# Attention and MLP on one core: the order of the first loads, with two w_out pieces and batch 1's first q and k between w_in's third and fourth piece

## The chip, the cores and the metric

The kernel runs on one core of a Trainium2 chip. A core has five engines with a queue of instructions each: TensorE (PE: matmuls, with PEld for its weight loads), VectorE (DVE), ScalarE (ACT), GpSimd (POOL) and SyncE (SP, which here issues nearly all DMAs). Each queue is worked off in order; semaphores make an instruction wait for another engine's or for a DMA. The metric is the device time of one execution in microseconds (us), less is better.

## The reference

Two layers in a row. The first is attention over 8 batches, 8 heads, 576 positions and 64 dimensions, with a window: heads 0 to 3 see the last 32 positions, heads 4 to 7 (dilated) every fourth of the last 128. The second takes the heads of a position as a row of 512 and applies two matrices with a leaky ReLU between them.

```
scores = where(mask[h], q @ k.T / 8, -1e9)        # rel = query - key
mask[h < 4]  = (0 <= rel < 32)
mask[h >= 4] = (0 <= rel < 128) & (rel % 4 == 0)
x   = softmax(scores) @ v                          # 8 x 8 x 576 x 64
x   = x.transpose(0, 2, 1, 3).reshape(4608, 512)
h   = x @ w_in                                     # 512 x 2048
out = maximum(0.01 * h, h) @ w_out                 # 2048 x 512
```

All inputs and the output are float32; the kernel computes in fp16 with float32 sums.

## The kernel before

The 4608 rows are worked in 12 chunks of 384 (three to a pair of batches). A chunk goes *up*: 16 blocks j of 128 hidden units, each four matmuls over the 512 inputs (`up`, L1112, matmuls at L1128), evicted by ACT with the leaky ReLU into `gt` (L1139). Then it goes *down*, 128 rows at a time. The first four row tiles are done plainly (`down`, L1288): four groups of four matmuls, 128x512 (L1299). All others go four tiles at a time in `group` (L1341), which computes a two by two block product with seven products for eight; its matmuls are L1390. The last four chunks do the same on the way up (`up_seven`, L1168, matmuls L1212). Both need sums and differences of weight quarters (`weight_sums`, L1325, with L1329 for w_out; `up_sums`, L1154, for w_in), 128x2048 each on DVE.

Batches 0 and 1 (`EARLY`) are done in a form of their own: q and k are loaded in rows, cast to fp16 (L345 on POOL and DVE, L343 on ACT), turned by PE (L783) and copied into `slots` (L698 on ACT, L700 on DVE). A `unit` (L896) then has scores (L924, L943, L927), an exponential on ACT (L949), for some a mask on DVE (L960), the product with the values (L984, L994, L1004, and L972 for the row sums), logarithm and exponential for the reciprocal (L1016, L1018) and the norm into `xt` (L1022). The first 512 positions of a batch are "part 0", the last 64 of each head the remainder ("part 1", loaded by `load_rest`, L544). Chunk 0 is batch 0's part 0, chunk 1 batch 1's, chunk 2 the two remainders. The other six batches (`late_unit`, L1031: scores L1065, mask L1081, sums and values L1071, norm L1100) are turned by DVE (L751, L771, L776) with copies on POOL (L739).

Weights come as float32 pieces of 512 KB (`load_w`, L611): w_in in eight, w_out in eight, each cast to fp16 by two or four casts. Pieces are staged in buffers that are used later for other things: w_in's first two in `gt[2]`, the third and fourth in `wst[0]`, then `gt[1]` and `xt[1]`; w_out's first in `xt[1]`, the second and third again in `wst[0]` (so they wait for the casts of w_in's third and fourth), the rest again in `gt[1]` and `xt[1]`. The first four pieces of w_in make the left half of the hidden units: pieces one and two the first two of the four input blocks, three and four the last two.

What sets the order is a planner that runs when the kernel is built. Every instruction is a task with a guessed duration for each engine that may take it (`add`, L84; loads with a guessed service time, `load`, L330). `_Plan.run` (L106) places tasks on engines by readiness and priority; `latest` (L169) goes backwards over the result and makes each task's due time its new priority, and the two are repeated once for each entry of `SEEDS`, an entry other than zero adding random shifts. The planned order is then fixed in every engine's queue. SP's loads keep a priority of their own: `FIRST` (L26) is a string that is read from left to right (L1518 to L1526): `b` and `c` are q and k of a group of four heads of batch 0 and 1, `v` and `y` their values, `i` a piece of w_in, `o` a piece of w_out, `0` and `1` the remainders. A load waits for what last used its buffer, and each of SP's DMAs also waits for the DMA eight places before it, for they share eight semaphores. Where the plan leaves PE idle before `WARM`, filler matmuls on zeros are put in (L1616; the first eight are at L1509).

These are the lines in which the list's costs of w_in's first pieces and of the remainder stand:

```
    def load(queue, dst, src, n, size, deps, prio, slow=1.0):
        ...
        return plan.dma(queue, 0.7 if n == 1152 else 0.62 if over == 64 else 0.45, took(n, size) * slow, deps,
...
        t = load("SP", st, dram(moe_w_in, n % 4 * 128 * DFF + x, [DFF, 128], [1, 1024]), 128, 4096, old, prio,
                 W_SLOW if n < 4 else 1.0)
```

`WHEN` and `RANKS` are first priorities of the batches' attention, `MOE` the pitch of the chunks' first priorities, `W_SUMS` and `SUMS` those of the weight sums.

Of the kernel before, what the change touches and what calls it, by code (L numbers as in the profile page):

```python
# [16 lines left out]
LATE = 7.0  # L17
HOLD = 5.0
W_ENG = ("POOL", "DVE", "ACT")
WHEN = (31.41, -0.6, 17.98, 85.1, 92.7, 99.49, 158.42, 166.15)  # L20
WARM = 62.0
W_SLOW = 1.5
SEEDS = (0, 0, 0, 0, 0, 0, 0, 0, 206472, 469597)
AFTER = -1495.0
NEAR = -1482.0
FIRST = "bvbviiii0iiiicoocoyoooooy1"  # L26
RANKS = ((24.53, -24.71), (34.17, 3.07), (0.12, 16.48), (29.7, 7.1))


def _constants():  # L30
# [47 lines left out]
class _Plan:  # L78
# [11 lines left out]
    def shared(self, *args):  # L90
        t = self.add(*args)
        t.port = True
        return t
# [117 lines left out]
def kernel(  # L211
# [43 lines left out]
    def at(tl, p0, p1, off, *dims):  # L255

        row = tl.ap[0][0]
        return bass.AP(tensor=tl.tensor, offset=tl.offset + p0 * row + off,
                       ap=[[row, p1 - p0]] + [list(d) for d in dims])

    def dram(t, off, *dims):
        return bass.AP(tensor=t.tensor, offset=t.offset + off, ap=[list(d) for d in dims])
# [67 lines left out]
    def load(queue, dst, src, n, size, deps, prio, slow=1.0):  # L330
        eng = ENG[queue]
        over = getattr(src if prio == -3000 else dst, "ap", [[0, 0]])[0][1]
        return plan.dma(queue, 0.7 if n == 1152 else 0.62 if over == 64 else 0.45, took(n, size) * slow, deps,
                        lambda e: eng.dma_start(dst, src), prio,
                        LATE if prio > -1500 + len(FIRST) else 0.8 if prio >= AFTER else 0.0)

    def cast(dst, src, n, deps, prio, engines=("POOL",)):
        cost = {"POOL": 0.05 + n * (0.00118 if n <= S else 0.00104), "DVE": 0.1 + n * 0.00053,
                "ACT": 0.06 + n * 0.00087}

        def fn(e):
            if e == "ACT":
                nc.scalar.copy(out=dst, in_=src)  # L343
            else:
                ENG[e].tensor_copy(out=dst, in_=src)  # L345
        return shared(tuple((e, cost[e]) for e in engines), None, 0.2, deps, fn, prio, 0.0, "cast")
# [6 lines left out]
    def ring(name, n, users):  # L353

        r = rings.setdefault(name, [])
        waits = r[-n] if len(r) >= n else []
        r.append(users)
        return (len(r) - 1) % n, waits
# [23 lines left out]
    def clear_slots(slots, prio, deps):  # L382
        for i in slots:
            t_zero[i] = ([clear("DVE", qbd[i][64:128, 0:S], 0.34, 0.0, prio, deps),
                          clear("DVE", qbd[i][0:64, S:2 * S], 0.34, 0.0, prio, deps)],
                         [clear("DVE", kt[i][:, 0:PAD], 0.1, 0.0, prio, deps)])
# [157 lines left out]
    def load_rest(b, prio):  # L544


        _, r_old = ring("REST", 1, r_users := [])
        sn, s_old = ring("STG", NST, s_users := [])
        st, lo = stg[sn], []
        for o, src in ((0, q), (1, k)):  # L550
            lo.append(load("SP", at(st, 0, 128, o * 256, [1, 256]),
                           dram(src, b * H * HS + 512 * D, [HS, 8], [4 * D, 16], [1, 256]),
                           128, 1024, s_old, prio, 1.8))
        c = cast(at(rest, 0, 128, 0, [128, 8], [D, 2], [1, D]),
                 at(st, 0, 128, 0, [D, 8], [0, 2], [1, D]), 1024, lo + r_old, prio, W_ENG)
        s_users.append(c)
        vs, v_old, v_users = v_late[b]
        spread = bass.AP(tensor=vs.tensor, offset=vs.offset + 1024,
                         ap=[[4 * vs.ap[0][0], 16], [256, 4], [1, 256]])
        lv = load("SP", spread,  # L560
                  dram(v, (b * H + 4) * HS + 512 * D, [4 * D, 16], [HS, 4], [1, 256]),
                  64, 1024, v_old + [t_vr], prio)
        if b in SEL:
            ps, p_old, p_users = v_late[b, "plain"]
            lp = [load("SP", at(ps, 0, 128, 1024 + 256 * i, [D, 4], [1, D]),
                       dram(v, b * H * HS + (352 + 96 * i) * D, [D, 128], [HS, 4], [1, D]), 512, 256, p_old, prio)
                  for i in range(2)]
            for j in range(2):
                vt, d_users = kept[b, j]
                c_p = cast(at(vt, 0, 128, 512, [768, 2], [128, 2], [1, D]),  # L570
                           at(ps, 0, 128, 1024 + D * j, [2 * D, 2], [256, 2], [1, D]), 256, lp + d_users, prio, W_ENG)
                p_users.append(c_p)
                picked[b, j, 2] = [c_p]
        for vi in (2, 3, 0, 1):
            vt, d_users = kept[b, vi]
            c_v = []
            if vi >= 2:
                c_v = [cast(at(vt, 0, 64, 0, [1024, 2], [128, 4], [1, D]),
                            at(vs, 0, 64, 1024 + (vi - 2) * 256, [512, 2], [D, 4], [1, D]), 512,
                            [lv] + d_users, prio + 30, W_ENG)]  # L580
                v_users += c_v
            visits[b, vi, 1] = rest, [c], r_users, vt, c_v + seen_ones[b, vi], d_users
# [28 lines left out]
    def load_w(n, prio):  # L611
# [6 lines left out]
        if n >= 8:  # L618
            x = 1024 * (n - 8)
            t = load("SP", st, dram(moe_w_out, 128 * x, [2 * DM, 128], [1, 1024]), 128, 4096, old, prio)  # L620
            for i in range(2):
# [6 lines left out]
        t = load("SP", st, dram(moe_w_in, n % 4 * 128 * DFF + x, [DFF, 128], [1, 1024]), 128, 4096, old, prio,  # L628
                 W_SLOW if n < 4 else 1.0)
        g, h = n % 4 // 2, n % 2  # L630
# [15 lines left out]

    segs = {b: [(0, 96, 384 * (b % 2)), (96, 48, 768 + 192 * (b % 2))] for b in range(EARLY)}
    chunks = [(m, 384 * i, 384) for m in range(B // 2) for i in (0, 1, 2)]
    MOE = 36.66
    PLAIN = 4  # L650
    tiles = [(c, tt) for c in range(len(chunks)) for tt in range(3)]
    groups = [tiles[i:i + 4] for i in range(PLAIN, len(tiles), 4)]
# [1 line left out]
    for m, x, n in chunks:  # L654
        begins.append(begins[-1] + MOE * n / 384)

# [488 lines left out]
        return t_p  # L1145

    SEVEN = (8, 9, 10, 11)
    W_SUMS = 539.34
    u_sums, u_last = {}, {}

    def w_quarter(k, f):
# [2 lines left out]
    def up_sums(old, raw):  # L1154
# [3 lines left out]
        def make(n, dst, x, y, op, deps):  # L1158
            u_sums[n] = shared("DVE", 1.16, 0.2, deps,
                            lambda e: ENG[e].tensor_tensor(out=dst, in0=x, in1=y, op=op),  # L1160
                            W_SUMS, 0.0, "T")
        w_all = [c for j in range(NJ) for b in w_in_t[j] for c in b]
# [154 lines left out]
    def w_block(k, n):  # L1317
        return at(w_out, 0, 128, k * HJ * DM + n * HN, [DM, HJ], [1, HN])

    def flat(tl):  # L1320
        return at(tl, 0, 128, 0, [HN, HJ], [1, HN])
# [3 lines left out]
    def weight_sums():  # L1325
        w_all = sum((w_out_t[j] for j in range(NJ)), [])

        def minus(n, dst, x, y, deps):
            t_sum[n] = shared("DVE", 1.16, 0.2, deps, lambda e: nc.vector.tensor_tensor(  # L1329
                out=dst, in0=x, in1=y, op=ALU.subtract), SUMS, 0.0, "T")  # L1330
        minus(1, flat(sums[1]), w_block(0, 1), w_block(0, 0), w_all + w_used[9] + w_used[10])
# [4 lines left out]

    roles = [0, 1]
    last_of = {}
    SUMS = -123.87

    def group(four, acts, at_time, split):  # L1341

# [175 lines left out]
    ranks = {}  # L1518
    for n, step in enumerate(FIRST):
        seen = FIRST[:n].count(step)  # L1520
        if step in "io":
# [14 lines left out]
    def attend(b, part, first, step):  # L1536
        units = {None: (0, 1), 0: (0, 1), 1: (2,)}[part]
        if part == 1:
            load_rest(b, ranks[b])
        for n, hp in enumerate((2, 3, 0, 1)):  # L1540
            if part != 1 and n % 2 == 0:
                load_group(b, hp // 2, *(ranks[b, hp // 2, i] if b < EARLY else tick()
                                         for i in (0, 1)))
            if part == 0 and b in SEL and hp == 0:
                for u in units:
                    pick_values(b, u, first + step * n)
            got = turn(b, hp, part or 0, first + step * n)
            for u in units:
                if part is None:
                    late_unit(b, hp, u, got, first + step * n)  # L1550
                else:
                    unit(b, hp, part, u, got, first + step * n)
# [3 lines left out]
    for m in range(B // 2):  # L1556
        for b in (2 * m, 2 * m + 1):
            if b < EARLY:
                attend(b, 0, *RANKS[2 * b])
                if b == 0:  # L1560
# [3 lines left out]
                    clear_slots(range(4, NT), -700, x_done[0, 0][-1:])  # L1564
                attend(b, 1, *RANKS[2 * b + 1])
            else:
                a, z = WHEN[b - 1], WHEN[b]
                attend(b, None, a, (z - a) / 4)
# [40 lines left out]
    order = plan.run()  # L1609
    for seed in SEEDS:  # L1610
        plan.latest(seed)
# [67 lines left out]
```

## Time and profile before

| | |
|---|---|
| median of 3 runs | 307.46 us (307.44 to 307.6) |
| the profiled execution | 307.5 us |
| its span, first to last instruction | 305.7 us |
| granted TensorE clock | 1.00 |
| PE busy | 293.6 us, 96% |
| DVE, ACT, POOL busy | 247.8, 223.9, 123.2 us |
| read from and written to HBM | 37.25 MB, 9.44 MB |

How to read it: a row of a timeline has the start in us, the time it took, engine, line, operation, tiles and shapes, how many instructions were merged, and in brackets the idle time before it and what ended it. Busy time of PE counts filler as well, and matmuls overlap in the pipeline: eight of 128x384 that stand in a row are busy for 1.46 us but take 1.30 us of the chain. The profile's order by time has the loads first (DMA at 277 to 405 GB/s up to 40 us), the two early batches and chunk 0 up to 60 us, and from 70 us on matmuls back to back.

### The profile page before, as it was taken

Reading aid. Unit: us, or ns where it says so; the run is one execution under the profiler, and the core shown is the slowest. Engines: PE = TensorE matmul, PEld = TensorE weight load, DVE = VectorE, ACT = ScalarE, POOL = GpSimd, SP = SyncE. Lnnn points to the kernel's source line nnn. Section 1 sums busy time; section 2 is a strip of 40 time slices with the busy share of each in tenths; the row PEclk is TensorE's granted clock in tenths of the full one; section 3 lists DMA queues with packets and bytes.
Section 4 is the critical chain, followed back from the end, with each engine's and each line's share of the span. In section 5 each row is a group of like instructions: output and inputs, shape, how many; then the busy total and the mean of one; then the engine's idle time right before and its main releaser. Section 6 shows DMA issues by size and latency. Waiting matters only on the chain.

```text
span 305.7 us, 8137 instructions
## 1 busy us (share of the span) xinstructions
PE 293.6 (96%) x3050; PEld 231.4 (76%) x3050; DVE 247.8 (81%) x480; ACT 223.9 (73%) x547; POOL 123.2 (40%) x170
## 2 busy tenths in 40 slices
PE   8788899899999999999999999999999999999994
PEld 4445564466989678778877778778999999999984
DVE  5777868656999987999997889999999568677842
ACT  5788995597897885876778688577878768767420
POOL 6355862139908908954944753781000000000000
PEclk9999999999999999999999999999999999999999
DMA  7999988799897897848794988791211310031034
GB/s 244 405 362 376 405 270 147 178 174 203 169 190 151 149 169 161 147 115 145 161 160 134 166 173 162 143 199 46 72 36 34 101 41 0 2 105 36 2 109 133
DMA packets 155671, 47.23 MB, mean 154 GB/s; under 512 B 135408, under 2 KB 153072, under 8 KB 155632
## 3 DMA queue, kind: packets, MB, share of 16 engines
q1 hardware_dynamic: 155056, 46.39, 63.4%
q8 instruction: 24, 0.39, 0.5%
q10 hardware_dynamic: 576, 0.32, 0.4%
q14 instruction: 15, 0.12, 0.1%
HBM read 37.25 MB, written 9.44 MB: 153 GB/s over the span
## 4 chain that ended last, share of the span: by engine, by line
PE 78%; ACT 10%; DVE 7%; DMA 2%; issue 2%; SPq 1%; ACTq 0%
PE hps L1128 22%; PE fps L1390 21%; PE tp L1390 8%; PE hps L1212 7%; PE ops L1071 4%; PE ops L1212 3%; PE fps L1299 3%; DMA stg<-in_q_dram 2%; ACT gt L1139 2%; PE sps L1212 2%; ACT slots L698 2%; ACT ee L949 2%; ACT rc L1016 1%; DVE ee L1081 1%; PE sps L1071 1%
## 5 line engine op out<-in xcount | busy, mean ns | idle before, releaser
L1128 PE MATMUL hps<-xt,w_in 128*128 128x384 f16 (+1 forms) x556 | 98.5, 307 | 0.8 <-ACT gt L1139 0.7
L1390 PEld LDWEIGHTS <-gt 128*128 128x128 f16 x768 | 72.6, 98 | 8.8 <-DVE gt L1376 0.2
L1139 ACT ACTIVATE gt<-hps 128x384 f16<-128x384 f32 (+1 forms) x139 | 62.9, 457 | 21.8 <-PE hps L1128 20.3
L1128 PEld LDWEIGHTS <-w_in 128*128 128x128 f16 x576 | 49.9, 98 | 22.3 <-issue 1.7
L1390 PE MATMUL fps<-w_out,gt 128*128 128x256 f16 x368 | 47.0, 272 | 0.0
L739 POOL COPY slots<-turned 64x512 f16<-64x512 f16 (+1 forms) x36 | 27.7, 769 | 42.8 <-DVE turned L751 30.3
L345 POOL CAST v_all<-vst 64x1152 f16<-64x1152 f32 (+4 forms) x30 | 35.2, 1175 | 8.8 <-DMA vst<-in_v_dram 8.4
L345 POOL CAST nat<-stg 128x576 f16<-128x576 f32 (+1 forms) x46 | 34.9, 783 | 6.9 <-DMA stg<-in_q_dram 3.3
L1100 DVE TENSOR_TENSOR xt<-ops,rc 128x288 f16<-128x288 f32 x48 | 26.7, 557 | 5.7 <-PE ops L1071 3.1
L1081 DVE TENSOR_TENSOR ee<-ee,late_m 128x384 f16<-128x384 f16 (+1 forms) x48 | 27.1, 575 | 3.8 <-ACT ee L1078 3.2
L1212 PEld LDWEIGHTS <-w_in 128*128 128x128 f16 x256 | 21.9, 98 | 0.4
L1092 ACT ACTIVATE rc<-rc 128x288 f32<-128x288 f32 x48 | 21.2, 449 | 0.5
L1419 ACT COPY stg<-fps 128x512 f32<-128x512 f32 (+1 forms) x25 | 13.4, 534 | 10.6 <-PE fps L1390 10.2
L771 DVE STREAM_TRANSPOSE slots<-nat 64x576 f16<-64x576 f16 x24 | 18.4, 768 | 0.4
L751 DVE STREAM_TRANSPOSE turned<-nat 128x576 f16<-128x576 f16 (+1 forms) x24 | 17.5, 734 | 0.7 <-POOL slots L739 0.5
L1071 PEld LDWEIGHTS <-v_all 128*128 128x128 f16 x240 | 14.4, 98 | 3.9 <-issue 0.9
L1071 PE MATMUL ops<-ee,v_all 128*128 128x96 f16 (+2 forms) x240 | 16.4, 199 | 0.6 <-DVE xt L1100 0.6
L1212 PEld LDWEIGHTS <-stg 128*128 128x128 f16 x192 | 16.5, 98 | 0.3
L1299 PE MATMUL fps<-w_out,gt 128*128 128x512 f16 x64 | 16.2, 379 | 0.6 <-DVE w_out L345 0.6
L1390 PE MATMUL fps<-wst,gt 128*128 128x256 f16 x128 | 16.4, 272 | 0.0
L1071 PEld LDWEIGHTS <-sides 128*128 128x128 f16 x240 | 13.8, 97 | 3.0 <-issue 0.3
L1390 PE MATMUL tp<-w_out,gt 128*128 128x256 f16 x120 | 15.6, 273 | 0.0
(159 smaller groups left out, 593.9 us busy)
## 6 DMA issues: line engine op xcount, KB each, us to landing
stg<-in_q_dram SPq DMA_DIRECT2D x48, 144.0 KB, 3.5
stg<-in_k_dram SPq DMA_DIRECT2D x48, 144.0 KB, 3.0
vst<-in_v_dram SPq DMA_DIRECT2D x12, 288.0 KB, 4.0
vst<-in_v_dram SPq DMA_DIRECT2D x26, 128.0 KB, 2.8
gt<-in_moe_w_in_dram SPq DMA_DIRECT2D x5, 512.0 KB, 6.7
xt<-in_moe_w_out_dram SPq DMA_DIRECT2D x3, 512.0 KB, 9.0
gt<-in_moe_w_out_dram SPq DMA_DIRECT2D x3, 512.0 KB, 9.0
out_dram<-osb SPq DMA_DIRECT2D x9, 128.0 KB, 2.1
```

What stands on the lines that cost most here:

```text
L345: ENG[e].tensor_copy(out=dst, in_=src)
L739: lambda e: (nc.scalar.copy if e == "ACT" else nc.gpsimd.tensor_copy)(out=at(to, p0, p1, p0 if to is qb else 0, *dims), in_=at(fr, p0, p1, ...
L771: lambda e, p0=64 * h: nc.vector.transpose(at(qb, p0, p0 + 64, p0, [128, 9], [1, 64]), na[p0:p0 + 64, S:2 * S]), prio))
L1071: nc.tensor.matmul(at(bk, 0, 128, o, *dims), stationary(s), et[:, c:c + n], start=i == 0, stop=i == len(parts) - 1, skip_group_check=True)
L1081: lambda e: nc.vector.tensor_tensor(out=et[:, 0:w], in0=et[:, 0:w], in1=mk, op=ALU.mult), prio + 0.1)
L1092: lambda e: nc.scalar.activation(out=rt[:, 0:NQ], in_=rt[:, 0:NQ], func=AF.Exp, scale=-1.0),
L1100: lambda e: nc.vector.tensor_tensor(out=dst, in0=at(ot, 0, 128, 0, *src), in1=at(rt, 0, 128, 0, *src), op=ALU.mult), prio + 0.2)
L1128: nc.tensor.matmul(ht[:, 0:n], at(w_in, 0, 128, i * DFF + j // 2 * 256 + j % 2, [2, 128]), at(xt[m % 2], 0, 128, i * 1152 + x0 + x, [1, n] ...
L1139: lambda e: nc.scalar.activation(out=gt[c % NG][:, j * n_c + x:j * n_c + x + n], in_=ht[:, 0:n], func=AF.Prelu, alpha=0.01),
L1212: nc.tensor.matmul(bk[:, 192 * jj:192 * jj + 192], w(i, 2 * jp + jj), x(i), start=first and jj == 0 and i == 0, stop=jj == 1 and i == 1, s ...
L1299: nc.tensor.matmul(ft, g[:, j * n_c + tt * 128:j * n_c + tt * 128 + 128], w_out[:, j * DM:j * DM + DM], start=(j == 0), stop=(j == NJ - 1))
L1390: nc.tensor.matmul(bk[:, x:x + HN], tl[:, off + j * step:off + j * step + 128], rhs(j), start=first and x == 0 and j == 0, stop=j == HJ - ...
```

## The change

Constants alone change. The string of loads is another one: after the third `i` come two `o`, one `c`, then the fourth `i` and the remainder of batch 0, and the rest of w_in and w_out alternate. On SP's queue as built, w_out's first piece and batch 1's q and k of the dilated heads stand ahead of w_in's fourth piece; w_out's second piece, which must wait for the casts of w_in's third, stands behind w_in's fifth. Batch 1's plain values stand ahead of w_out's last two pieces, no longer behind them. The list's cost of w_in's first four pieces goes from 1.5 to 1.05 of the common one, that of the remainder's q and k from 1.8 to 1.2. First priorities and seeds are others too, so that the planned order differs on all engines from some 10 us on; the last 20 us or so of PE's order are the same.

```
-WHEN = (31.41, -0.6, 17.98, 85.1, 92.7, 99.49, 158.42, 166.15)
+WHEN = (69.34, -4.31, -32.5, 87.5, 98.94, 115.0, 145.55, 161.66)
 WARM = 62.0
-W_SLOW = 1.5
-SEEDS = (0, 0, 0, 0, 0, 0, 0, 0, 206472, 469597)
+W_SLOW = 1.05
+SEEDS = (0, 0, 0, 0, 0, 38627, 255542)
...
-FIRST = "bvbviiii0iiiicoocoyoooooy1"
-RANKS = ((24.53, -24.71), (34.17, 3.07), (0.12, 16.48), (29.7, 7.1))
+FIRST = 'bvbviiiooci0ioiioooicyyoo1'
+RANKS = ((24.19, -10.83), (18.59, -5.85), (-22.74, -9.73), (19.79, 2.61))
...
             lo.append(load("SP", at(st, 0, 128, o * 256, [1, 256]),
                            dram(src, b * H * HS + 512 * D, [HS, 8], [4 * D, 16], [1, 256]),
-                           128, 1024, s_old, prio, 1.8))
+                           128, 1024, s_old, prio, 1.2))
...
-    MOE = 36.66
+    MOE = 19.48
...
-    W_SUMS = 539.34
+    W_SUMS = 174.3
...
-    SUMS = -123.87
+    SUMS = -285.6
```

## The prediction

> **What bounds the kernel now.** The page first, for the busiest engine:
>
> ```profile
> PE 293.6 (96%) x3050; PEld 231.4 (76%) x3050; DVE 247.8 (81%) x480; ACT 223.9 (73%) x547; POOL 123.2 (40%) x170
> ```
>
> TensorE (PE) is busy for 96% of the span, so a gain can only come from where it waits or idles on filler. The table by stretches finds that (PE, PEld, DVE, ACT, POOL busy; then clock, DMA share, GB/s):
>
> ```profile
> 80.00:90.00 10.00, 9.45 (x140) 8.65 (x138) 9.87 (x16) 8.77 (x30) 4.57 (x5) 1.00 0.89 177
> 160.00:180.00 20.00, 20.00 (x230) 15.63 (x227) 16.54 (x31) 15.76 (x38) 11.22 (x14) 1.00 0.71 152
> 200.00:220.00 20.00, 20.00 (x245) 17.10 (x244) 19.91 (x34) 15.84 (x39) 6.60 (x8) 1.00 0.40 104
> ```
>
> After 70 us PE misses 0.55 us here and 0.27 us in 100:120, and nothing else before the tail: there is nothing to gain late. The opening, cut at two events, with the fillers (L1616) of the first two stretches below (PE and PEld alone):
>
> ```profile
> 22.00:44.80 22.80, 20.66 (x179) 12.45 (x178) 17.14 (x47) 20.96 (x49) 15.41 (x29) 1.00 1.03 366
> 44.80:60.30 15.50, 13.76 (x107) 6.86 (x106) 11.41 (x26) 9.37 (x29) 3.44 (x7) 1.00 0.76 155
> 60.30:75.50 15.20, 15.20 (x116) 9.41 (x115) 10.08 (x24) 12.96 (x29) 9.38 (x15) 1.00 1.01 187
> ...
> 22.00:44.80 22.80, 1.71 (x6) 0.39 (x4) 1.00 1.03 366
> 44.80:60.30 15.50, 1.19 (x4) 0.38 (x4) 1.00 0.76 155
> ```
>
> From 22 to 44.8 us ScalarE (ACT) is busy 20.96 of 22.80 us: it paces PE. From 44.8 to 60.3 PE works 13.76 - 1.19 = 12.57 us of 15.50, so 2.9 us are waits and filler. The timelines give the events: PE, then ACT, POOL, DVE.
>
> ```profile
> 1.00 3.59 PE L1509 MATMUL fps<-warm 128*128 128x512 f16 x8 [1.00 <-POOL warm L349]
> 14.49 1.05 PE L596 MATMUL sps<-osb,turned 128*128 128x256 f16 x8 [1.41 <-ACT osb L343]
> 20.62 1.58 PE L1616 MATMUL fps<-warm 128*128 128x512 f16 x7
> 22.64 0.74 PE L1128 MATMUL tp<-xt,w_in 128*128 128x384 f16 x3 [0.28 <-DVE xt L1022]
> 60.35 1.46 PE L1128 MATMUL hps<-xt,w_in 128*128 128x384 f16 x8
> ...
> 23.89 0.48 ACT L1139 ACTIVATE gt<-tp 128x384 f16<-128x384 f32 x1
> 45.97 0.48 ACT L949 ACTIVATE ee<-sps 128x384 f16<-128x384 f32 x1
> ...
> 13.92 0.61 POOL L345 CAST w_in<-gt 64x512 f16<-64x512 f32 x1 [1.57 <-DMA gt<-in_moe_w_in_dram]
> 15.13 0.61 POOL L345 CAST w_in<-gt 64x512 f16<-64x512 f32 x1 [0.60 <-DMA gt<-in_moe_w_in_dram]
> 16.38 0.61 POOL L345 CAST w_in<-wst 64x512 f16<-64x512 f32 x1 [0.63 <-DMA wst<-in_moe_w_in_dram]
> 18.26 0.74 POOL L345 CAST w_in<-wst 64x512 f16<-64x512 f32 x1 [1.27 <-DMA wst<-in_moe_w_in_dram]
> ...
> 49.98 1.22 DVE L1329 TENSOR_TENSOR wst<-w_out 128x2048 f16<-128x2048 f16 x1
> 80.23 1.98 DVE L1329 TENSOR_TENSOR w_out<-w_out 128x2048 f16<-128x2048 f16 x1
> ```
>
> Chunk 0 of the up product starts at 22.64 us, released by the norm of batch 0; chunk 1 starts at 60.35 us (call it T1). w_in's first pieces land 1.21, 1.25 and 1.88 us apart.
>
> **The change part by part.** The sums, matmuls and bytes are the same; the order differs. The costs told to the list (1.05 for 1.5, 1.2 for 1.8), MOE, WHEN, RANKS, SEEDS and the two due times act through the order alone.
>
> 1. *w_in's fourth piece.* One w_out piece and batch 1's first q and k (512 KB each) pass it on SP's queue. At 379 GB/s (stretch 20:30) 512 KB take 1.38 us, at the piece interval 1.25. It lands at 16.38 + 1.25 + 2 x 1.38 + 1.25 = 21.6 us; if all four took 1.88 us, at 23.9. I take 22.0, since three of the four intervals resemble the shorter rows. The eight first ups are reordered: 14 matmuls that need pieces one to three alone stand first, 14 x 0.163 = 2.3 us (eight take 1.30 in the chain), from 22.9 to 25.2. 0.3 of that start is new: VectorE (DVE) now casts batch 1's q (0.41) ahead of the last norms. DVE reaches the fourth piece's casts at 24.0 (norms to 22.8, clears 1.2) and ends them at 24.8 even if it lands at 23.9, so PE does not wait. The price is ACT's: it gets its first finished bank at 25.75, not 23.89.
>
> 2. *ACT to the fifth exponential of batch 1.* Before, 49 instructions stand from that bank to this exponential (45.97): 22.1 us, some 1.3 of it waits. The new order has 48, by kind 0.2 us less (a v cast 0.39 and a mask copy 0.48 out; a logarithm 0.3 and longer copies 0.36 in). The fifth falls between 25.75 + 20.6 = 46.3 and 25.75 + 21.9 = 47.6; I take 46.9: **0.9 us later**. Later w_in pieces land some 4 us later and w_out3's issue on SP waits for their casts; batch 1's v is queued behind that issue (my walk: 31.0, four us ahead of its turn). On POOL a mask copy that waits for ACT now stands ahead of one w_in cast; such a wait took 2.9 us before (41.86 on POOL). That cast ends at 36.1 in the walk and serves ups twelve to fifteen, due near 39. All this hides behind batch 0's remainder, batch 1's early transposes and two w_out groups now near 32 and 34 us, where PE had filler. Without that cover each us late is a us on ACT.
>
> 3. *From there to T1.* Before: 60.35 - 45.97 = 14.4 us. By the order PE has six groups of four L1299 matmuls left before T1, not ten: -4 x 0.866 = -3.5. So with the same waits 10.9. Floor: DVE must finish the last norms; its 11.41 us in this stretch lose one L1329 (1.22, now behind T1) and some 1.2 net of casts: 9.0. I walked the new order with the old durations (ACT: three exponentials, eight logarithm steps, a cast of the remainder; then copies and norms) and got 9.8; two waits of 0.25 more, 10.3. T1 = 57.2, **3.15 us earlier**.
>
> 4. *What was put off.* Two L1299 groups now stand behind T1: 2 x 0.87 = **+1.73**.
>
> 5. *T1 to the first late batch.* Before, its scores come 15.2 us after T1 (60.3 to 75.5), with PE full. New cover is one group longer (0.87). New on POOL is one mask (no row shows it there; the nearest, casts of 128x512 and 64x1152, take 0.61 and 1.14); new on DVE the L1329, 1.22. A gain is excluded, since PE has no idle time here. So between 0 and 1.2; I take 0.3, as the added cover pays 0.87.
>
> The Trainium skill (SBUF — State Buffer, Who interferes with whom) says that a DVE operation with two SBUF inputs and a GpSimd one that reads SBUF block each other; the 1.98 against 1.22 of the two L1329 rows, the slow one beside POOL casts, agrees. By that rule, with POOL's mask beside it, this L1329 would take 0.76 more and the sum come to -0.3.
>
> 6. *Late batches.* Reordered throughout, same work. At best it saves the 0.8 us above; at worst see below. I take 0.
>
> Sum: T1 -3.15, put off +1.73, step 5 +0.3 = **-1.1 us**. The profiled run took 307.5 (span 305.7 and 1.8 around it), the median of the runs 307.46: forecast 306.4. Ends: T1 at 46.3 + 9.0 = 55.3 gives -3.3; T1 at 47.6 + 10.9 = 58.5 and 1.2 in step 5 gives +1.1.
>
> **The rivals.**
> - *Slower, w_in's last casts late.* Chunk 0's ups eight to fifteen need w_in's last piece; DVE casts it behind seven copies of turned q and k, which alternate with ACT's. In the table of waits such copies waited
>
> ```profile
> DVE slots L700 <- ACT slots L698: 6.9, 14, 0.7
> ```
>
>   0.5 us each. My walk has those casts end at 34.8 (before: 33.1) with three such waits; if four more come, ACT's later evictions all shift by 2.0: -1.1 + 2.0 = +0.9, 308.4. It decides from 1.7 us on. For: ACT has no slack there. Against: filler and two w_out groups stand in between, and ACT has other work queued. Chance 0.20.
> - *Slower, new waits late.* DVE is busy 19.91 of 20 us in 200:220; a less lucky order makes every late batch wait as 80:90 does. Five more times 0.55 = 2.75, less 0.27: -1.1 + 2.5, 308.9. For: that stretch; against: PE is full in all others. Chance 0.14.
> - *Same.* T1 comes earlier but batch 2's chain (POOL casts, DVE transposes, loads) does not, and PE gives 1.1 us back at its scores: 307.5. For: in 60:75 POOL waits on DVE; against: DVE is free for 5 us there. Chance 0.16.
> - *Faster yet.* The waits before T1 all but vanish, the end of the sum: -3.3, 304.2. For: the two w_out groups fill what was filler; against: DVE's 9.0 us leave no slack. Chance 0.08.
> - *Clock.* PE's first eight matmuls take 3.59 us, seven later ones 1.58: half pace at first. A long gap near 30 us, where the first w_out group waits for late casts, could bring half pace back: as many slow rows again lose 3.59 / 2 = 1.8, and the gap itself more than the 1.41 us at 14.49, after which no row is slow. -1.1 + 3.2 = +2.1, 309.6. Chance 0.02.
>
> The Trainium skill (TensorE: Matmul & The Clock Gate, Why this matters for your kernels) warns of PE gaps above about 3 us; no row here has one.
>
> **How the numbers follow.** The forecast, 305.2 to 306.8, has 0.40. 0.2% (0.6 us) is about what a measurement of this kernel can tell from no change. Faster 0.40 + 0.08 = 0.48, same 0.16, slower 0.20 + 0.14 + 0.02 = 0.36. The range 304.4 to 309.0 reaches to the two slower rivals and most of the way to the lower end.
>
> **What would show it.** Right: L1128's first rows near 22.9, ACT's first L1139 near 25.7, chunk 1's first up near 57, late scores near 74. Wrong: a PE wait on a w_in cast near 25 or 35, T1 after 58.6, or PE under 9.5 of 10 us in several stretches after 70.

## The result and the profile after

The changed kernel takes 306.42 us (median of 22 runs, 305.13 to 308.25) against 307.46 us before (22 runs on the same chip): the ratio is 0.9969, with a 95% interval of 0.9958 to 0.9981, so about 1 us less. In a later comparison the ratio was 0.9969 again (0.9948 to 0.9990), with medians of 306.90 and 307.43. The ratio is not the quotient of the two medians, which is 0.9983 there; here and in the table below the verdicts go by the ratio and its interval. The profiled execution of the changed kernel took 307.11 us (span 305.3), 0.7 above its median; the one before took 307.5, its median. The two traces thus show 0.4 us of the 1.0, and a second trace of the changed kernel (306.79 us, span 305.0) is used beside the first.

Of the page of the changed kernel, the line of busy time; then its table by stretches, cut as before (PE, PEld, DVE, ACT, POOL busy; clock, DMA share, GB/s); below, fillers alone (L1616, PE and PEld) in the first two stretches.

```profile
PE 291.6 (96%) x3047; PEld 230.2 (75%) x3047; DVE 250.1 (82%) x480; ACT 222.4 (73%) x544; POOL 126.4 (41%) x173
```

```profile
22.00:44.80 22.80, 19.77 (x163) 11.46 (x161) 18.69 (x47) 19.03 (x45) 15.97 (x29) 1.00 1.02 344
44.80:60.30 15.50, 14.43 (x131) 7.86 (x130) 11.89 (x27) 11.71 (x34) 5.99 (x10) 1.00 0.95 190
60.30:75.50 15.20, 15.20 (x119) 9.19 (x117) 10.08 (x24) 12.31 (x29) 9.86 (x16) 1.00 0.96 187
80.00:90.00 10.00, 9.54 (x144) 9.02 (x142) 9.50 (x19) 8.66 (x28) 3.47 (x4) 1.00 0.91 173
200.00:220.00 20.00, 20.00 (x238) 16.86 (x237) 19.05 (x36) 15.09 (x36) 5.65 (x8) 1.00 0.32 92
...
22.00:44.80 22.80, 2.12 (x8) 0.45 (x6) 1.00 1.02 344
44.80:60.30 15.50, 0.39 (x1) 0.10 (x1) 1.00 0.95 190
```

From 22 to 44.8 us PE does less than before (19.77 - 2.12 = 17.65 us of work, before 20.66 - 1.71 = 18.95), and ACT, busy 20.96 of 22.80 us before, is now busy only 19.03: it waits more. From 44.8 to 60.3 PE does more: 14.43 - 0.39 = 14.04 us for 12.57. From 60.3 to 75.5 PE is as full as before. The two w_out groups near 32 and 34 us, chunk 1's first up (T1) and the first late scores stand on PE's timeline as follows; then ACT's, POOL's and DVE's rows that the prediction named.

```profile
22.39 0.69 PE L1128 MATMUL hps<-xt,w_in 128*128 128x384 f16 x2
31.50 0.59 PE L1299 MATMUL fps<-w_out,gt 128*128 128x512 f16 x2
32.49 0.59 PE L1299 MATMUL fps<-w_out,gt 128*128 128x512 f16 x2 [0.39 <-DVE w_out L345]
34.23 1.02 PE L1299 MATMUL fps<-w_out,gt 128*128 128x512 f16 x4
37.78 0.32 PE L924 MATMUL sps<-con 128*128 128x384 f16 x1 [1.14 <-ACT ee L949]
58.46 1.46 PE L1128 MATMUL hps<-xt,w_in 128*128 128x384 f16 x8
74.50 0.34 PE L1065 MATMUL sps<-slots 128*128 128x96 f16 x5
...
25.40 0.49 ACT L1139 ACTIVATE gt<-tp 128x384 f16<-128x384 f32 x1 [0.17 <-PE tp L1128]
32.01 0.58 ACT L698 COPY slots<-tp 64x512 f16<-64x512 f16 x1 [0.84 <-DVE slots L700]
48.33 0.55 ACT L698 COPY slots<-tp 64x480 f16<-64x480 f16 x1 [0.75 <-DVE slots L700]
48.78 0.48 ACT L949 ACTIVATE ee<-sps 128x384 f16<-128x384 f32 x1
...
22.99 0.61 POOL L345 CAST w_in<-wst 64x512 f16<-64x512 f32 x1 [1.20 <-DMA wst<-in_moe_w_in_dram]
...
24.39 1.17 DVE L345 CAST w_in<-wst 64x512 f16<-64x512 f32 x2
30.00 1.52 DVE L345 CAST w_in<-gt 64x512 f16<-64x512 f32 x2
31.55 0.43 DVE L700 COPY slots<-tp 64x512 f16<-64x512 f16 x1
```

T1 comes at 58.46 us, 1.89 earlier (in the second trace at 57.84, 2.51 earlier). The first late scores come at 74.50, 1.03 earlier, with one w_out group (0.87 us) fewer done ahead of them than before. Two such groups, 1.73 us, were put off behind T1 in all. So of the 1.89 us the opening keeps 0.16 in this trace, and 2.51 - 1.73 = 0.78 in the second.

To count the same thing over a whole trace, the following sections use "PE lost": the time from each matmul's start to the next one's, less the usual step of its line and shape in the trace before, plus all filler. Only its differences are used: its absolute size hangs on what is taken as the usual step. Before, PE lost 25.3 us up to 80 us and 2.6 after it; in the two traces of the changed kernel 25.2 and 24.6 up to 80 us, 2.3 and 2.8 after it.

### The profile page after: what moved, and what is told of

Same layout as the page of the kernel before. It is cut to its first block, busy times and chain, and to the rows that moved or that the text cites. A ratio compares the mean times of both kernels' runs of the same rounds, so it can differ in the third digit from the quotient of the medians.

```text
span 305.3 us, 8148 instructions
## 1 busy us (share of the span) xinstructions
PE 291.6 (96%) x3047; PEld 230.2 (75%) x3047; DVE 250.1 (82%) x480; ACT 222.4 (73%) x544; POOL 126.4 (41%) x173
## 4 chain that ended last, share of the span: by engine, by line
PE 84%; ACT 5%; DVE 5%; DMA 2%; issue 1%; POOL 1%; SPq 1%; POOLq 0%; ACTq 0%
PE hps L1128 24%; PE fps L1390 22%; PE tp L1390 8%; PE hps L1212 7%; PE ops L1071 4%; PE ops L1212 3%; PE fps L1299 3%; DMA vst<-in_v_dram 2%; PE sps L1212 2%; PE sps L1071 1%; DVE slots L700 1%; PE sps L1065 1%; PE ops L1065 1%; PE ops L1390 1%; ACT w_in L343 1%
## 5 line engine op out<-in xcount | busy, mean ns | idle before, releaser
L1139 ACT ACTIVATE gt<-hps 128x384 f16<-128x384 f32 (+1 forms) x139 | 62.5, 457 | 28.2 <-PE hps L1128 27.2
L739 POOL COPY slots<-turned 64x512 f16<-64x512 f16 (+1 forms) x36 | 26.7, 744 | 51.3 <-DVE turned L751 38.8
L345 POOL CAST v_all<-vst 64x1152 f16<-64x1152 f32 (+4 forms) x31 | 36.6, 1185 | 6.1 <-DMA vst<-in_v_dram 5.6
L345 POOL CAST nat<-stg 128x576 f16<-128x576 f32 (+1 forms) x47 | 35.9, 784 | 3.3 <-PE ops L972 0.9
L1081 DVE TENSOR_TENSOR ee<-ee,late_m 128x384 f16<-128x384 f16 (+1 forms) x48 | 25.3, 537 | 4.3 <-ACT ee L1078 3.9
L1212 PEld LDWEIGHTS <-w_in 128*128 128x128 f16 x256 | 21.8, 98 | 0.3
L1419 ACT COPY stg<-fps 128x512 f32<-128x512 f32 (+1 forms) x24 | 12.8, 532 | 10.3 <-PE fps L1390 9.2
L1376 DVE TENSOR_TENSOR gt<-gt 128x1024 f16<-128x1024 f16 x21 | 16.3, 779 | 0.3 <-PE fps L1390 0.2
```

The source lines that it names most:

```text
L739: lambda e: (nc.scalar.copy if e == "ACT" else nc.gpsimd.tensor_copy)(out=at(to, p0, p1, p0 if to is qb else 0, *dims), in_=at(fr, p0, p1, ...
L1081: lambda e: nc.vector.tensor_tensor(out=et[:, 0:w], in0=et[:, 0:w], in1=mk, op=ALU.mult), prio + 0.1)
L1139: lambda e: nc.scalar.activation(out=gt[c % NG][:, j * n_c + x:j * n_c + x + n], in_=ht[:, 0:n], func=AF.Prelu, alpha=0.01),
L1212: nc.tensor.matmul(bk[:, 192 * jj:192 * jj + 192], w(i, 2 * jp + jj), x(i), start=first and jj == 0 and i == 0, stop=jj == 1 and i == 1, s ...
```

## The experiments

Three theories were tried. A: the gain is made in the opening, by what all engines do there, and not by the place of the loads alone. B: the place of w_out's first piece and batch 1's q and k ahead of w_in's fourth piece is the gain. C: each new planning throws the late batches about, and the gain is what came up. Line numbers in some of the kernels are shifted by added lines.

| kernel | median us | ratio to before (95%) | T1 | late scores | PE lost to 80 us | after 80 us |
|---|---|---|---|---|---|---|
| before | 307.46 | 1 | 60.35 | 75.53 | 25.3 | 2.6 |
| after | 306.42 | 0.9969 (0.9958 to 0.9981) | 58.46 | 74.50 | 25.2 | 2.3 |
| after, second trace | 306.90 | 0.9969 (0.9948 to 0.9990) | 57.84 | 73.88 | 24.6 | 2.8 |
| loads alone | 308.41 | 1.0040 (1.0019 to 1.0061) | 61.99 | 77.17 | 27.0 | 2.6 |
| fourth piece back | 306.64 | 0.9977 (0.9959 to 0.9995) | 57.81 | 73.85 | 24.5 | 2.3 |
| string alone | 311.14 | 1.0127 (1.0106 to 1.0149) | 59.43 | 75.60 | 27.2 | 4.2 |
| string of before | 306.55 | 0.9990 (0.9965 to 1.0014) | 56.35 | 71.53 | 21.3 | 5.0 |
| opening of after, late of before | 306.12 | 0.9954 (0.9936 to 0.9971) | 58.38 | 75.30 | 25.1 | 2.0 |
| opening of before, late of after | 307.03 | 0.9986 (0.9972 to 1.0000) | 60.36 | 75.54 | 25.7 | 1.9 |
| opening of "string of before", late of after | 303.93 | 0.9883 (0.9860 to 0.9906) | 57.23 | 72.40 | 22.5 | 2.6 |
| told costs alone | 306.90 | 0.9978 (0.9965 to 0.9991) | 57.00 | 69.81 | 21.8 | 5.1 |
| two ACT copies more | 308.15 | 1.0028 (1.0011 to 1.0045) | 60.15 | 76.18 | 26.9 | 2.3 |
| four casts on DVE | 307.07 | 0.9977 (0.9959 to 0.9996) | 58.47 | 74.51 | 25.2 | 2.4 |
| w_in ahead of w_out | 306.07 | 0.9959 (0.9941 to 0.9977) | 58.00 | 70.80 | 23.6 | 2.8 |

The last four columns come from one profiled execution each. Those of "loads alone" (309.71 us) and "four casts on DVE" (307.64 us) were the longest of their kernels. What stands behind the start of the last matmul is in none of the columns; it took 3.6 to 4.6 us in these traces, 4.1 before, 4.2 and 4.0 in the two of the changed kernel, and differed between executions whose late order is the same. Late scores is the first late scores matmul on PE; how much other work stands ahead of it differs between plannings, so only the lost time can be compared across them.

**The loads alone, and the fourth piece alone.** In the kernel before, only SP's order is changed; in the changed kernel, only w_in's fourth piece goes back.

```
+    put_ahead([w_load[8]] + qk_load[1, 1], w_load[3])
...
+    put_ahead([w_load[3]], w_load[8])
```

The first line goes into the kernel before, the second into the changed one, each behind the planning. `w_load[3]` is w_in's fourth piece, `w_load[8]` w_out's first, `qk_load[1, 1]` batch 1's q and k of the dilated heads.

> The order of PE, ACT, DVE and POOL is that of before; on SP alone, w_out's first piece and batch 1's first q and k are put ahead of w_in's fourth piece. Theory A (the gain comes from what the engines do with the early pieces, so all orders have to change): w_in's fourth piece lands some 3 us later, near 21.5 us, which the first ups of before, who need it from about 23 us on, feel by 0 to 0.8 us; no gain: 307.4 to 308.3, T1 (chunk 1's first up) at 60.3 to 61.2. Rival B (the place of the loads on SP's queue is what gains): about 1 us less, 306.4, T1 near 58.5.

> The changed kernel, with w_in's fourth piece alone put back ahead of w_out's first piece and batch 1's q and k on SP's queue. Theory A: the gain does not hang on this place; its casts on DVE stand where they stood (24.4 us), the three other loads are needed later than they land, so the time stays that of the changed kernel within 0.3: 306.1 to 306.8. Rival B: the gain is given back, 307.2 to 307.6.

The first is slower by 0.4%, 0.1 us above the upper edge of theory A's interval. Its PE timeline and the casts that it waits for:

```profile
22.94 0.32 PE L1129 MATMUL tp<-xt,w_in 128*128 128x384 f16 x1 [0.28 <-DVE xt L1023]
24.38 0.62 PE L1129 MATMUL tp<-xt,w_in 128*128 128x384 f16 x2 [1.11 <-ACT w_in L343]
...
23.71 1.14 ACT L343 CAST w_in<-wst 64x512 f16<-64x512 f32 x2 [1.22 <-DMA wst<-in_moe_w_in_dram]
```

The order of before wants the fourth piece from its third matmul on; it lands near 23.7, and PE stands 1.11 us, more than the 0.8 that was expected. T1 at 61.99 is late for theory A too, but this execution was 1.3 us longer than the kernel's median. The second kernel is as fast as the changed one: the place of that load neither gives nor takes anything that can be told once the engines' order expects it late. Rival B falls on both.

**The string alone, and the string of before.** Both are planned again.

```
-FIRST = "bvbviiii0iiiicoocoyoooooy1"
+FIRST = 'bvbviiiooci0ioiioooicyyoo1'      # in before, nothing else
...
-FIRST = 'bvbviiiooci0ioiioooicyyoo1'
+FIRST = "bvbviiii0iiiicoocoyoooooy1"      # in after, nothing else
```

> The kernel before, with the changed string of loads alone (FIRST); due times, seeds and costs as before, and the list planned again. Theory A: the order of the opening follows from the string, so a part of the gain comes: 306.4 to 307.4, T1 at 58.5 to 60. Rival C (which order the seeds happen to give decides, whatever the string): anything from 306 to 310, with T1 and the time after T1 apart from both known kernels.

> The changed kernel with the string of loads of before; its due times, seeds and costs stay. Theory A: w_out's first piece comes too late for the two w_out groups near 32 and 34 us and T1 falls back: 307.0 to 308.5, T1 after 59.5. Rival C: anything from 306 to 310, and T1 says nothing of the time.

Theory A failed on both. With the new string alone T1 was in its range, but the time was 3.7 us above it, and 1.1 us above even the range of rival C. With the old string both the time and T1 were earlier than theory A had them; rival C's range holds there. The new string alone is 1.3% slower, with 1.8 us more lost in the opening and 1.6 more late. With the old string the changed kernel's opening gets better still: 21.3 us lost, four less than before, but 5.0 are lost late. The largest piece of that is one wait for a DVE operation on `gt`, in 120:130:

```profile
121.71 1.46 PE L1128 MATMUL hps<-xt,w_in 128*128 128x384 f16 x8
124.69 0.50 PE L1390 MATMUL tp<-w_out,gt 128*128 128x256 f16 x3 [1.52 <-DVE gt L1376]
```

So an opening and a late part come out of every planning, each good or bad, and a total says little of either. That asked for a graft.

**Grafts.** Tasks and their dependences are the same in all these kernels; only order and engine differ. Each engine was given one kernel's order up to the first late scores and another's for the rest.

```
-    order = plan.run()
-    for seed in SEEDS:
-        plan.latest(seed)
-        order = plan.run()
...
+    raw = zlib.decompress(base64.b85decode("".join(ORDER)))
```

`ORDER` is a packed list: all tasks that one planned order starts before the first late scores, then all other tasks as another planned order has them.

> Every engine's order is that of the changed kernel up to the first late scores, and that of before for all that is then left. Theory A (the gain is made in the opening, T1 earlier): most of the gain stays, 306.3 to 306.9, T1 as in the changed kernel, 57.8 to 58.5. Rival C (the gain is made after 70 us, by another order of the late batches): it is gone, 307.2 to 308.

> The other half: the order of before up to the first late scores, that of the changed kernel after them. Theory A: no gain but the 0.3 us that the late stretches lose less, 307.0 to 307.5, T1 at 60.3. Rival C: the gain is here, 306.2 to 306.8.

> The opening of the run with the old string of loads and the changed due times and seeds (T1 at 56.35, first late scores at 71.53), and behind it the changed kernel's order of the late batches. Up to 80 us PE lost 21.3 us in that run and 25.2 in the changed kernel, after 80 us 5.1 and 2.3. Theory A (what the opening gains stays, if the late order has its cover): 306.4 - 3.8 = 302.6, from 302.2 to 303.6. Rival (the late batches' own chain of loads, copies and turns does not come earlier and gives it back as waits between 80 and 130 us, as in that run): 305.0 to 306.5.

> The changed kernel once more, beside the three others on the same chip, for a second trace of it. All theories: 306.1 to 306.8; T1 between 57.8 and 58.5.

By the times, the opening of the changed kernel alone brings 1.3 us, no less than the whole change (0.2 better than expected); its late order alone brings 0.4, with an interval that reaches 0. The two intervals of the ratio just do not overlap. That is theory A, with at most a small share for C; the gains don't add up (1.3 + 0.4 against 1.0). The traces show less of it. Up to 80 us the five with this opening (the two of the changed kernel, "fourth piece back", "opening of after, late of before", "four casts on DVE") lose 24.5 to 25.2 us, 24.9 on the average; the two with the opening of before lose 25.3 and 25.7, and 0.3 of the latter stand where the two orders meet. So the opening gains some 0.5 us in these traces. After 80 us one and the same late order lost 2.6 us in one execution and 2.0 in another (that of before), or 1.9 to 2.8 (that of the changed kernel), so no gain of the late order can be told in the traces. Where the rest of the 1.0 us stands is open. In the second trace of the changed kernel, 0.6 of the 2.8 us lost late stand at 160 to 180 us, where the first trace lost 0.04; why such a loss comes in some executions is open.

The third graft beats both kernels, by 3.5 us or 1.2% against before. Six of its seven runs took 303.07 to 305.41 us; the seventh took 307.65, with a mean granted clock of 0.989. It missed its interval by 0.3 us: its opening lost 22.5 us, not 21.3, and 0.3 of this is at the seam, where the two orders meet (70:80 us). Its opening stretches and the place of the wait above:

```profile
22.00:44.80 22.80, 21.17 (x187) 13.19 (x186) 19.25 (x54) 22.03 (x57) 15.51 (x30) 1.00 1.04 372
44.80:60.30 15.50, 15.01 (x130) 8.10 (x129) 10.41 (x24) 10.66 (x32) 3.22 (x7) 1.00 0.83 174
...
120.00:130.00 10.00, 10.00 (x91) 7.47 (x89) 9.96 (x14) 5.95 (x15) 7.38 (x9) 1.00 0.61 121
```

ACT is busy 22.03 of 22.80 us here, where the changed kernel has 19.03: this is what an opening with few waits of ACT looks like.

**The told costs alone, and another string.** In before only the two costs are changed; in after only the second part of the string.

```
-W_SLOW = 1.5
+W_SLOW = 1.05
...
-                           128, 1024, s_old, prio, 1.8))
+                           128, 1024, s_old, prio, 1.2))
```

```
-FIRST = 'bvbviiiooci0ioiioooicyyoo1'
+FIRST = 'bvbviiiooci0iiiioooocyyoo1'
```

> The kernel before with the two told costs alone (1.05 for w_in's first pieces, 1.2 for the remainder), the list planned again; string, due times and seeds of before. If the told costs carry the gain: 306.0 to 306.9, T1 at 57.5 to 59. If they do nothing by themselves: 307.0 to 308.0 with T1 near 60. Rival C (any new planning throws the late batches about): up to 311, with the loss after 80 us, not T1.

> The changed kernel with another string: its first part stays (two w_out pieces and batch 1's q and k ahead of w_in's fourth piece), but the rest of w_in comes ahead of the rest of w_out; planned again. With the old string under the same due times TensorE lost 21.3 us up to 80 us, with the new one 24.6. If the alternation of w_in's second half with w_out is what costs those 3 us: 21.5 to 22.7 here, T1 at 56 to 57, and the time 303.5 to 305 if the late order is no worse. If the early w_out pieces and q and k are: 24 to 25 here, T1 after 57.5, 306 or more.

The told costs alone gain 0.2%: 3.5 us less lost in the opening (T1 at 57.00, 0.5 earlier than expected), 2.5 given back late. The other string gives 306.07. Its time and T1 (58.00) are those of the second case, that the early w_out pieces and q and k cost the opening; its lost time (23.6) lies between the two cases, so the run leans to the second and does not settle it. Lost time up to 80 us by the two parts of the change:

| | costs of before | new costs |
|---|---|---|
| string of before | 25.3 | 21.8; 21.3 with the new due times and seeds |
| new string | 27.2 | 25.2 and 24.6; 23.6 with w_in ahead |

In each row the new costs gain 2 to 4 us, in each column the new string loses about as much. But in the lower row the right cell has the new due times and seeds as well, and no run has the new string and the new costs without them. Each cell has one or two planned orders, so luck of planning is not excluded as a part of it.

**ACT, and VectorE's long casts.** Two copies of 128x480 more on ACT at 35.2 us; and two casts of batch 1's q and k moved from POOL to DVE.

```
+    first = late_mask[0]
+    for i in range(2):
+        w = _Task((("ACT", 0.0),), 0.0, [], lambda e: nc.scalar.copy(out=scratch, in_=con[:, 0:480]), 0, 0.0, 0, "w")
```

The copies stand ahead of the mask copy `first`. The second edit is again a packed `ORDER`, that of the changed kernel, in which the four casts `nat<-stg` at 38 to 42 us stand on DVE instead of two on POOL and two on DVE.

> The changed kernel with two copies of 128x480 more on ScalarE (a scratch tile, some 0.5 us each, 1.0 to 1.1 in all) ahead of the mask copy that stands at 35.2 us. If ScalarE paces TensorE there, as the prediction's second step has it, T1 and the time move by all of it: T1 58.8 to 59.0, 307.4 to 307.9. If TensorE and VectorE share the lead there: half or less, 306.5 to 307.1.

> The changed kernel with batch 1's other two casts of the plain q and k (POOL, 38.26 and 39.38 us) moved to VectorE, beside the two that stand there. In all four traces of the changed opening a VectorE cast of 128x512 at 38.3 to 38.9 takes 2.27 us where such casts take 0.43, beside casts that POOL does back to back. If that is what makes the fifth exponential late: the four casts end near 40.1 and not at 41.1 although VectorE does twice as many, the fifth exponential comes at 47.2 to 47.6 and not at 48.15, T1 at 56.9 to 57.4, the time 305.4 to 306.1. If the delay has cover: T1 stays at 57.8 and the time at 306.4 within 0.3. If VectorE's two more casts cost it what they take: T1 58.3, 306.9.

The ACT copies, an exponential behind them, the fifth exponential of batch 1 and PE's wait; then the page's row of the granted clock (a digit for each 7.7 us, in tenths), and a row of PE with these copies and the same one in the second trace without them:

```profile
35.15 1.22 ACT L1645 COPY scratch<-con 128x480 f16<-128x480 f16 x2
37.69 0.49 ACT L950 ACTIVATE ee<-sps 128x384 f16<-128x384 f32 x1
50.45 0.48 ACT L950 ACTIVATE ee<-sps 128x384 f16<-128x384 f32 x1
...
38.23 0.32 PE L925 MATMUL sps<-con 128*128 128x384 f16 x1 [2.25 <-ACT ee L950]
...
PEclk9999979999999999999999999999999999999999
...
40.25 1.80 PE L1129 MATMUL hps<-xt,w_in 128*128 128x384 f16 x5
...
38.59 0.98 PE L1128 MATMUL hps<-xt,w_in 128*128 128x384 f16 x5
```

The exponential behind the copies comes 1.07 us later than in the second trace (37.69 against 36.62), which is what the copies take; PE's wait on it doubles, from 1.14 to 2.25. The delay reaches PE in full: up to here ACT does pace it.

The fifth exponential of batch 1 then comes 2.30 later (50.45 against 48.15) and T1 2.31. ACT's copies are not shown to be the cause of this second part. In this trace the granted clock of TensorE was 0.5 from 39.0 to 42.4 us, and PE's rows there took up to about twice as long (1.80 us for 0.98); 1.2 of the 2.3 us arise in these rows and just behind them, and ACT now waits for PE (0.31, 0.19 and 0.50 us, where the second trace has 0.17 once). The times go the same way. Of this kernel's 12 runs, the five with a mean granted clock of 0.998 or more took 307.29 to 308.06 us (median 307.65), the seven with 0.989 to 0.994 took 308.08 to 309.71 (median 309.05). The five are 0.75 us above 306.90 and 1.23 above 306.42, at most what the copies take, and within the range that was expected if ACT paces PE.

The moved casts changed nothing that can be told: T1 58.47 as in the first trace, a ratio of 0.9977 beside 0.9969. They did not end sooner either (four on DVE from 38.98 to 41.89; two on DVE in the first trace from 38.91 to 41.75), so none of the three cases came as told. Whether the long cast would matter if it went away stays open.

## Why the prediction was right, point by point

The forecast was 306.4 and the measured time 306.42. That they meet so closely is luck. The way and the mechanism of most steps were right, but step 2 was 1.8 to 2.2 us too small; steps 1, 3 and 5 were too large by 0.3 to 0.6 each and made up for 1.3 to 1.4 us of it. The sums of the measured terms are -0.5 and -0.6 us in the two traces of the changed kernel, and its 22 runs lie between 305.13 and 308.25.

1. *w_in's fourth piece: near the forecast.* Casts from 22.99 us, so it landed up to 1.0 later than the forecast 22.0 and within its bounds; DVE's casts at 24.39 (24.0); first finished bank on ACT at 25.40 (25.75); of PE, only two weight loads waited for the casts, 0.22 and 0.31 us. That this load is not what decides is shown by putting it back.

2. *ACT to the fifth exponential of batch 1: the step that failed, in its size.* Forecast 46.9 with an upper bound of 47.6; measured 48.78 and 48.15. The work on ACT from first bank to that exponential was right: 20.1 us against 20.3 before (0.2 less, as counted). The waits were not: counting every gap, 3.26 and 2.82 us, where before had 1.79. The prediction had counted 1.3 there, and its upper bound left the waits as they were before: no term stood for more waits in the new order. The waits of ACT in that stretch, before and after:

```profile
ACT slots L698 <- DVE slots L700: 1.5, 5, 0.5
```

```profile
ACT slots L698 <- DVE slots L700: 2.6, 5, 0.8
```

The rows above name the place: DVE does two casts of w_in from 30.00 to 31.52, its copy of turned q or k follows at 31.55, and ACT's copy, which takes turns with it, waits 0.84. That is the mechanism that the prediction kept for its slower rival, w_in's late casts and the alternating copies; the rival looked for the last casts to be late for PE, while what came was that the casts stand in DVE's queue ahead of copies that ACT needs.

No run took these casts away, but six traces hold the pair, and its time differs from trace to trace: 0.85 (ACT copies put in), 1.17 ("opening of after"), 1.18 (second trace), 1.18 ("fourth piece back"), 1.52 (first trace) and 1.63 us ("four casts on DVE"). ACT's wait behind it was 0.18, 0.49, 0.50, 0.50, 0.84 and 0.95 us: always the pair's time less 0.67 or 0.68. So the casts do set this wait. It is 0.84 of the 1.46 us by which ACT's waits grew in the first trace and 0.50 of the 1.03 in the second. The rest is spread: 0.27 more ahead of the fifth exponential (0.75 us at 48.33, for 0.48 of before), 0.24 in the three short copies at 28 us, 0.17 for PE at 44.70.

3. *From there to T1: right.* 9.68 and 9.69 us against 10.3 (bounds 9.0 to 10.9). Together with step 2, T1 came 1.89 to 2.51 us earlier, not 3.15; of five traces with this opening (the six above without the ACT copies) two have T1 near 57.8 and three near 58.4. What tells these apart is the end of that pair of casts on DVE: it ends at 30.87 to 31.57 us in the five, and T1 comes 26.90 to 26.95 us behind it in each. In the first trace the pair starts 0.28 us later than in the second and takes 0.34 longer, which is the 0.62 between their T1. Why the pair takes longer in some executions is open. T1 in the first trace is 0.14 us short of the 58.6 that the prediction named as a sign of being wrong.

4. *Two groups behind T1, +1.73: right.* The stretch from T1 to the late scores holds one more, 16.04 us for 15.18, a difference of 0.86, and the second follows.

5. *T1 to the late scores: 0, not +0.3.* The 0.86 is the one group; nothing else was lost. DVE and POOL at T1:

```profile
58.14 1.22 DVE L1329 TENSOR_TENSOR wst<-w_out,wst 128x2048 f16<-128x2048 f16 x1
59.27 1.07 DVE L960 TENSOR_TENSOR ee<-ee,con 128x384 f16<-128x384 f16 x1
...
58.39 1.74 POOL L960 TENSOR_TENSOR ee<-ee,con 128x384 f16<-128x384 f16 x1 [0.97 <-ACT ee L949]
```

The new mask on POOL, which no row of before priced, took 1.74 us, and the L1329 beside it its usual 1.22. The price that the Trainium skill (SBUF — State Buffer, Who interferes with whom) seemed to put on this L1329, 0.76 us, was paid by POOL and by DVE's next mask, 1.07 us for a usual 0.36. That section of the Trainium skill has the operation that starts second blocked, and here the mask started second: the trace agrees, and the prediction had put the price on the wrong engine. From T1 to the late scores PE waits for neither.

6. *Late batches: 0, measured -0.3 to +0.2* in lost time, and 0.4 us of gain for the late order by itself, with an interval that reaches 0.

With the measured terms of the first trace: -1.89 + 1.73 + 0 - 0.3 = -0.5, which is 307.0 from 307.5 (that execution took 307.11). Of the second: -2.51 + 1.73 + 0 + 0.2 = -0.6, which is 306.9 (it took 306.79). With the trace of the kernel with the fourth piece back, which has the same order on four engines: -2.54 + 1.73 - 0.35 = -1.2, which is its 306.27. The median lies between these. What stands behind the last matmul's start is not in the sums; it was 0.5 us shorter in that last trace than before, so its close fit is partly chance. Of the rivals, "new waits late" is what three of the four other plannings got (4.2 to 5.1 us lost after 80 us, for 2.6), but not the changed kernel; "batch 2's chain gives it back" did not come, since no PE wait stands at the late scores; the longest PE gap behind the start was 1.14 us in both traces of the changed kernel, and the granted clock stayed at 1.00 there. With the ACT copies, though, PE stood for 2.25 us from 36 us on, less than the 3 us that the prediction names, and half clock followed: what the clock rival feared can come in this kernel.

What the prediction did not see is that the two told costs and the string pull in opposite ways. It took the costs as acting "through the order alone", which is true, and so gave them no term; by the table above, as far as one or two plans in a cell can tell, they are the larger part of the opening's gain, and the string takes most of it back.

## What to carry to other kernels

Where a planner makes the order, a constant's effect is the sum of several parts of the span that move independently: take each part's lost time on the busiest engine, and graft the best opening onto the best rest (here 3.5 us, where the change had 1.0). When an engine paces a stretch, count its waits in the new order and not its work alone: look for the operations that alternate with another engine, and for what now stands ahead of them in that engine's queue. Here a load's place in its queue was worth nothing by itself; the order of the engines that use it had to expect it there. When work is put in to test which engine paces a stretch, look at the granted clock before reading the delay: here half of it arose while the clock was halved.

## What the runs showed of the hardware

A DVE cast of 128x512 from float32 took 2.27 us in the second trace, against 0.43 for others of its shape. POOL did four operations back to back meanwhile. DVE first (the first of the row's two took 2.27 us), then POOL:

```profile
38.29 2.83 DVE L345 CAST nat<-stg 128x512 f16<-128x512 f32 x2
41.77 0.43 DVE L345 CAST w_out<-gt 128x512 f16<-128x512 f32 x1
...
38.26 0.61 POOL L345 CAST nat<-stg 128x512 f16<-128x512 f32 x1
38.82 0.61 POOL L345 CAST w_out<-wst 128x512 f16<-128x512 f32 x1
39.38 0.61 POOL L345 CAST nat<-stg 128x512 f16<-128x512 f32 x1
39.94 0.34 POOL L376 COPY late_m<-late_m 128x192 f16<-128x192 f16 x1
```

It was so in each of the five traces with these casts in this place (2.27 or 2.28 us): the DVE operation was not held up by one POOL operation but until POOL's run of four came to its end, and POOL's rows were not slowed. With half of POOL's casts moved away, the first DVE cast there took 1.16 us: POOL then had a cast and a copy back to back, and in all six traces the DVE cast ended 0.28 or 0.29 us behind the last of POOL's casts and copies in the row. That POOL is the cause is read from these times.

TensorE's clock can be halved in the middle of a kernel. In the trace with the two ACT copies PE stood still for 2.25 us up to 38.23, by far the longest gap in any trace here (the next is 1.52, with no loss of clock behind it), and the granted clock was 0.5 from 39.0 to 42.4 us. That the gap is the cause is not shown: five of that kernel's 12 runs kept a mean clock of 0.998 or more, and only one of the 12 was traced.
